# Gated linear attention into a squared-ReLU layer: k and q transposed by DMA from the fourth unit on, and the front of each unit issued ahead of the back of its predecessor

## Chip, cores, metric

One core of one Trainium2 chip. Its engines go by the names of the profile: PE (TensorE), PEld (PE's weight loads), DVE (VectorE), ACT (ScalarE), POOL (GpSimd) and SP, whose queue issues the DMAs. The releaser of a wait is what ended it. The metric is the device time of one execution in microseconds; the kernel before takes 197.5 us (median of 3 runs, 196.7 to 198.2).

## The reference

```python
# attention: 4 batches, 8 heads, 768 steps, head dimension 48
for t in range(S):
    state = alpha[:, :, t, :, None] * state + einsum('bhd,bhe->bhde', k[:, :, t], v[:, :, t])
    y[:, :, t] = einsum('bhd,bhde->bhe', q[:, :, t], state)
x = y.transpose(0, 2, 1, 3).reshape(3072, 384)
# layer ("MoE" in the code, one expert)
out = square(maximum(x @ w_in, 0)) @ w_out        # 384 -> 2048 -> 384
```

## The kernel before

The recurrence is done in chunks. A *unit* is 256 steps of one batch: 128 partitions, two steps (`j`) per partition, the halves of the partitions being two chunks (`ab`). There are 12 units, and for each an equal slice of the layer. Every operation is given to a list scheduler with a modelled cost, a priority and the buffers that it reads and writes; the scheduler fixes one order for each engine, and the engines then run in that order and wait by semaphores.

Within one unit: alpha's halves are multiplied (DVE), logarithm (ACT), a matmul with a triangle sums the columns (PE), exponentials (ACT) scale k and q (DVE), k and q are transposed on PE into a PSUM bank and copied out (DVE), scores (PE), mask (DVE), product with v and with the carried state (PE), then the output is transposed (PE) into the layout that the layer needs.

```python
psH = [128, 2, 512] FP32     # layer, first product: 2 banks
psP = [128, 2, 512] FP32     # scores, and the column sums: 2 banks
psO = [128, 512] FP32        # layer, second product
psT = [128, 1024] BF16       # every transpose: 1 bank
psY = 2 x [128, 512] FP32

def attention(u):
    # ... alpha's halves multiplied (DVE, line 485), logarithm into the single buffer lab (ACT, 487)
    def m1(pe):                                              # column sums, into the score banks
        pe.matmul(psP[:, 0, 0:HD], LBLK[:], lab)
        # ... five small ones
    # ... exponentials of psP into asb (ACT, 512)
    for t in range(2):                                       # t = 0: k, t = 1: q
        # ... qks[t] = raw[t] * asb[t]  (DVE, 522)
        def tr(pe, t=t):                                     # 8 transposes (PE, 533)
            pst = psT[:, :].rearrange("p (n a j s) -> p n a j s", n=NPR, a=2, j=2)
            for j in range(2):
                for p in range(NPR):
                    ins = pe.matmul(pst[:, p, :, j, :], QKS[qs][:, t, j, 2*p:2*p+2, :]..., IDENT[:], is_transpose=True)
        add("pe", tr, ...)
        add("dve", copy psT -> KQT[kt][:, t], 640, ...)      # line 540
    # ... kv: new state (PE, 551; DVE, GpSimd)
    # ... score: 2 x 16 matmuls of 64x64 into psP (PE, 586); mask (DVE, 593)
    def y(pe):
        # carried state: 128-column stationary, one matmul per head pair and chunk (605)
        pe.matmul(psY[ab][:, p*96:p*96+96], KQT[kt][:, 1, p, ab, :], st[:, p*96:p*96+96], ...)
        # ... 32 matmuls with v (612)
    # ... output out of psY (ACT, 624), 6 transposes into psT (PE, 630), copy (DVE, 636)

for u in range(U):
    if u >= NRAW: loads(u)
    attention(u)                 # the order in which operations are told decides who waits for whom
for m in range(U):
    moe(m, [2*m, 2*m+1])
```

Of the kernel before, what the change touches and what calls it, by code (L numbers as in the profile page):

```python
# [4 lines left out]
AF = mybir.ActivationFunctionType  # L5
FP32 = mybir.dt.float32
BF16 = mybir.dt.bfloat16
# [275 lines left out]
def act_ns(n):  # L283
    return 65 + n * 0.8333
# [6 lines left out]
def bass_gla_recurrent__then__act_relu_squared_kernel(  # L291
# [9 lines left out]
    B, H, S, D = q.shape  # L301
    HD = H * D
    DM, DFF = moe_w_in.shape
    assert H == 8 and D == 48 and DM == HD and B % 2 == 0
    C = 128
# [3 lines left out]
    NPR = H // 2  # L309
    DP = 64  # L310
    HP = C // 2
    units = [(b, c) for c in range(0, NCH, 2) for b in range(B)]
    U = len(units)
    G = 2 * U

    NRAW, NVR, NLAB, NASB, NQKS, NKQT, NPM, NV, NXB, NRR, NGT, NOSB = 3, 3, 1, 2, 2, 2, 4, 2, 4, 4, 4, 3

    def sb(name, shape, dt, n):
        return [nc.alloc_sbuf_tensor(f"{name}{i}", shape, dt) for i in range(n)]
# [4 lines left out]
    LAB = sb("lab", [128, 2, H, DP], BF16, NLAB)  # L324
    ASB = sb("asb", [128, 2, HD], BF16, NASB)
    QKS = sb("qks", [128, 2, 2, H, DP], BF16, NQKS)
    KQT = sb("kqt", [128, 2, NPR, 2, C], BF16, NKQT)
    PM = sb("pm", [128, 2, 2, 2 * C], BF16, NPM)
    VBF = sb("vbf", [128, 2, HD], BF16, NV)
    SBD = sb("sbd", [128, HD], BF16, 2 * B)  # L330
# [2 lines left out]
    ACM = sb("acm", [128, 2, H], FP32, 2)  # L333
    XBF = sb("xbf", [128, HD], BF16, NXB)
    XT = nc.alloc_sbuf_tensor("xt", [128, KT, G * C], BF16)
    LBLK = nc.alloc_sbuf_tensor("lblk", [128, 128], BF16)
# [18 lines left out]
    psH = nc.alloc_psum_tensor("psH", [128, 2, 512], FP32)  # L355
    psP = nc.alloc_psum_tensor("psP", [128, 2, 512], FP32)
    psO = nc.alloc_psum_tensor("psO", [128, 512], FP32)
    psT = nc.alloc_psum_tensor("psT", [128, 1024], BF16)
    psY = [nc.alloc_psum_tensor(f"psY{i}", [128, 512], FP32) for i in range(2)]

    pr = Program(nc)
    add = pr.add
    P = 7000.0
# [96 lines left out]
    def loads(u):  # L460
        b, c = units[u]
        t0 = c * C
        r, vr = u % NRAW, u % NVR
        for o, (dst, t, nm, key) in enumerate(((RAW[r][:, 2, :, :], alpha, "a", ("raw", r, 2)),
                                               (RAW[r][:, 0, :, :], k, "k", ("raw", r, 0)),
                                               (RAW[r][:, 1, :, :], q, "q", ("raw", r, 1)),
                                               (RAV[vr][:], v, "v", ("rav", vr)))):
            src = t[b, :, t0:t0 + 2 * C, :].rearrange("h (p j) d -> p h (j d)", j=2)
            chain("sp", lambda e, dst=dst, src=src: e.dma_start(dst, src), 400, 2 * u * P - 4 * P + o, writes=[key],  # L469
                name=f"ld{nm}{u}", dma=f"{nm}{vr if nm == 'v' else r}", lag=1240)  # L470

    def attention(u):
        b, c = units[u]
        t0 = c * C
# [6 lines left out]
        def heads(t):  # L481
# [13 lines left out]
        add("pool", lambda e: e.tensor_tensor(q0, q0, heads(RAL[0][:]), ALU.mult), 1000, pu + 520,  # L495
            reads=[("raw", r, 1), ("ral",)], writes=[("raw", r, 1)], name=f"mq{u}")

        def m1(pe):
            pe.matmul(psP[:, 0, 0:HD], LBLK[:], lab)
            col = psP[:, 0, HD:HD + 2 * H]  # L500
            pe.matmul(col, HSEL[:], HCOL[:], start=True, stop=False, skip_group_check=True)
            col = col.rearrange("p (a n) -> p a n", a=2)
            for p in range(NPR):
                ins = pe.matmul(col[:, :, 2 * p:2 * p + 2],  # L504
                                LAB[la][:, 0, 2 * p:2 * p + 2, :].rearrange("p h d -> p (h d)"), ONES4[:],
                                start=False, stop=True, skip_group_check=True)
            return ins

        add("pe", m1, pe_ns(HD) + 135, pu + 300,
            reads=[("lab", la), ("lblk",), ("ones",), ("hsel",), ("hcol",)], writes=[("ps", "P")], name=f"m1_{u}")  # L510
        for t, sc in ((0, -1.0), (1, 1.0)):
            add("act", lambda e, t=t, sc=sc: e.activation(ASB[a][:, t, :], psP[:, 0, 0:HD], AF.Exp, scale=sc),  # L512
                act_ns(HD), pu + 500 + t, reads=[("ps", "P")], writes=[("asb", a, t)], name=f"e{t}{u}")
        add("act", lambda e: e.activation(ACM[u % 2][:].rearrange("p a n -> p (a n)"), psP[:, 0, HD:HD + 2 * H],
                                          AF.Exp), 110, pu + 505, reads=[("ps", "P")],
            writes=[("acm", u % 2)], name=f"ec{u}")
        add("act", lambda e: e.activation(VBF[vb][:].rearrange("p j (h d) -> p h j d", h=H),  # L517
                                          RAV[vr][:].rearrange("p h (j d) -> p h j d", j=2), AF.Copy), act_ns(2 * HD), pu + 600,
# [2 lines left out]
        for t in range(2):  # L521
            add("dve", lambda e, t=t: e.tensor_tensor(  # L522
                QKS[qs][:, t, :, :, 0:D].rearrange("p j h d -> p h j d"),
                RAW[r][:, t, :, :].rearrange("p h (j d) -> p h j d", j=2),
                bass.AP(tensor=ASB[a], offset=t * HD, ap=[[2 * HD, 128], [D, H], [0, 2], [1, D]]), ALU.mult),
                1100, pu + 1500 + 400 * t, reads=[("raw", r, t), ("asb", a, t)], writes=[("qks", qs, t)],
                name=f"qk{t}{u}")

            def tr(pe, t=t):
                pst = psT[:, :].rearrange("p (n a j s) -> p n a j s", n=NPR, a=2, j=2)  # L530
                for j in range(2):
                    for p in range(NPR):
                        ins = pe.matmul(pst[:, p, :, j, :],  # L533
                                        QKS[qs][:, t, j, 2 * p:2 * p + 2, :].rearrange("p h d -> p (h d)"),
                                        IDENT[:], is_transpose=True)
                return ins

            add("pe", tr, pe_ns(*[128] * 8), pu + 2500 + 600 * t, reads=[("qks", qs, t), ("ident",)],
                writes=[("ps", "T")], name=f"tr{t}{u}")
            add("dve", lambda e, t=t: e.tensor_copy(KQT[kt][:, t, :, :, :].rearrange("p n a s -> p (n a s)"),  # L540
                                                    psT[:, :]), 640, pu + 3000 + 600 * t,
                reads=[("ps", "T")], writes=[("kqt", kt, t)], name=f"et{t}{u}")

        halves = range(1 if last else 2)

        def kv(pe):
# [28 lines left out]
        for hp in range(2):  # L575
            pm = (2 * u + hp) % NPM
            pb, key = (psH, [("ps", "H", 0), ("ps", "H", 1)]) if u == 0 and hp else (psP, [("ps", "P")])

            def score(pe, hp=hp, pb=pb):
                for i in range(2):  # L580
                    p = 2 * hp + i
                    for j in range(2):
                        for ab in range(2):
                            for h in range(2):
                                ro = slice(64 * h, 64 * h + 64)
                                ins = pe.matmul(pb[ab * HP:(ab + 1) * HP, h, (2 * i + j) * C:(2 * i + j + 1) * C],  # L586
                                                KQT[kt][ro, 0, p, ab, j * HP:(j + 1) * HP],
                                                KQT[kt][ro, 1, p, ab, :])
                return ins

            add("pe", score, 340, pu + 3800 + 10 * hp, reads=[("kqt", kt, 0), ("kqt", kt, 1)], writes=key,
                name=f"p{hp}{u}")
            add("dve", lambda e, pm=pm, pb=pb: e.tensor_tensor(  # L593
                PM[pm][:].rearrange("p h i s -> p (h i) s"),
                pb[:, :, :].rearrange("p h (i s) -> p (h i) s", i=2),
                bass.AP(tensor=MASK, offset=0, ap=[[2 * C, 128], [0, 4], [1, 2 * C]]), ALU.mult), 1170, pu + 4200,
                reads=key + [("mask",)], writes=[("pm", pm)], name=f"pm{hp}{u}")

        def y(pe):
            for ab in range(2):  # L600
                if first and ab == 0:
                    continue
                st = SBA[u % 2] if ab else SBD[old]
                for p in range(NPR):
                    pe.matmul(psY[ab][:, p * 96:p * 96 + 96], KQT[kt][:, 1, p, ab, :], st[:, p * 96:p * 96 + 96],  # L605
                              start=(p == 0), stop=False, skip_group_check=True)
            for h in range(H):
                pm = PM[(2 * u + h // 4) % NPM]
                for j in range(2):
                    for ab in range(2):  # L610
                        ro = slice(ab * HP, (ab + 1) * HP)
                        ins = pe.matmul(psY[ab][:, h * D:(h + 1) * D], pm[ro, h % 2, (h // 2) % 2, j * C:(j + 1) * C],  # L612
                                        VBF[vb][ro, j, h * D:(h + 1) * D],
                                        start=(first and ab == 0 and h == 0 and j == 0), stop=(j == 1),
                                        skip_group_check=True)
            return ins
# [91 lines left out]
    for step in ("u0", "u1", "i0", "i1", "i2", "i3", "o0", "o1", "o2", "o3", "u2"):  # L708
# [4 lines left out]
            w_in_piece(i, -1e5 + i)  # L713
        else:
            w_out_piece(i, -1e5 + 10 + i)
    for u in range(U):
        if u >= NRAW:
            loads(u)
        attention(u)
    for m in range(U):  # L720
        moe(m, [2 * m, 2 * m + 1])
    pr.schedule()
# [30 lines left out]
```

## Time and profile before

| | before |
|---|---|
| span of the profiled run | 194.2 us |
| PE busy / not busy | 185.8 / 8.4 us |
| PE not busy from 38 to 76 us | 1.3 us |
| steady unit | 14.37 us, PE without a gap |
| DMA queue: bytes, share of 16 engines | 29.89 MB, 51.9% |

The rows come from the page (busy times, DMA queue) and from the busy time by stretch; the steady unit is the distance of two starts of the product with v, 101.96 and 116.33 us. The prediction shows the other lines. Those of the operations removed, from the groups by line (engine, operation, out<-in, shapes, count, then busy us, mean ns, idle before and releaser):

```profile
L540 DVE COPY kqt<-psT 128x1024 bf16<-128x1024 bf16 x24 | 16.5, 686 | 5.8 <-PE psT L533 5.6
...
L533 PE MATMUL psT<-ident,qks 128*128 128x128 bf16 x192 | 14.7, 219 | 0.3 <-DVE qks L522 0.3
```

### The profile page before, as it was taken

To read this page: it belongs to the slowest core of one execution; us is meant where nothing else is said; L and a number is where in the kernel's file an instruction comes from. 1 tells how busy PE (TensorE), PEld (TensorE's weight loads), DVE (VectorE), ACT (ScalarE), POOL (GpSimd) and SP (SyncE) were. 2 spreads that over 40 slices of the span, in tenths; PEclk is the share of its full clock that TensorE was granted. 3 is DMA by queue.
4 is the path that set the end of the run, shared out by engine and by line. 5 is a ranking of instruction groups with operands and counts; after the bars stand their busy time and mean duration, and the time that the engine had idled before them with its cause. 6 is when DMAs were issued, how large, how long until landed. Compare 5 with 4: busy or idle time off the path is not lost.

```text
span 194.2 us, 5455 instructions
## 1 busy us (share of the span) xinstructions
PE 185.8 (96%) x2347; PEld 132.8 (68%) x2347; DVE 117.9 (61%) x172; ACT 129.5 (67%) x252; POOL 86.1 (44%) x97
## 2 busy tenths in 40 slices
PE   7999899899998999999999999999999999999994
PEld 2455676675775678778778778777777677687762
DVE  6698644795983875855855855836736727622230
ACT  2647898696777488658658559559459458277642
POOL 8243785272471473743742742822812812325000
PEclk9999999999999999999999999999999999999999
DMA  6999999999994670950950940910110110110112
GB/s 161 323 367 384 378 365 254 261 291 315 296 316 117 178 230 3 243 165 3 241 167 0 263 146 5 271 55 1 43 43 3 40 44 0 44 40 3 40 40 81
DMA packets 57111, 30.23 MB, mean 156 GB/s; under 512 B 50432, under 2 KB 55552, under 8 KB 57088
## 3 DMA queue, kind: packets, MB, share of 16 engines
q1 hardware_dynamic: 57088, 29.89, 51.9%
q8 instruction: 18, 0.29, 0.6%
q14 instruction: 5, 0.04, 0.1%
HBM read 25.17 MB, written 4.72 MB: 154 GB/s over the span
## 4 chain that ended last, share of the span: by engine, by line
PE 70%; DMA 11%; SPq 9%; ACT 4%; POOL 2%; DVE 1%; issue 1%
PE psH L663 27%; PE psO L693 26%; SPq L469 8%; DMA stg<-in_moe_w_in_dram 5%; PE psT L533 4%; DMA raw<-in_alpha_dram 3%; DMA rav<-in_v_dram 3%; PE psP L586 3%; PE psY L551 2%; PE psY L612 2%; PE psT L630 2%; PE psY L605 1%; PE psH L693 1%; POOL gt L679 1%; ACT rr L672 1%; SPq L435 1%
## 5 line engine op out<-in xcount | busy, mean ns | idle before, releaser
L679 POOL TENSOR_TENSOR gt<-rr 128x512 bf16<-128x512 bf16 x45 | 48.3, 1074 | 68.3 <-ACT rr L672 68.3
L663 PE MATMUL psH<-xt,win 128*128 128x256 bf16 x576 | 73.0, 273 | 1.1 <-ACT rr L672 1.1
L693 PE MATMUL psO<-wout,gt 128*128 128x384 bf16 x368 | 69.6, 326 | 1.1 <-ACT osb L701 0.7
L672 ACT ACTIVATE rr<-psH 128x512 bf16<-128x512 f32 x96 | 56.5, 600 | 16.2 <-PE psH L663 15.4
L663 PEld LDWEIGHTS psH<-xt,win 128*128 128x128 bf16 x576 | 53.4, 98 | 11.6 <-ACT rr L672 2.0
L693 PEld LDWEIGHTS psO<-wout,gt 128*128 128x128 bf16 x368 | 33.9, 98 | 19.8 <-ACT osb L701 0.9
L593 DVE TENSOR_TENSOR pm<-psP,mask 128x1024 bf16<-128x1024 f32 x23 | 28.1, 1220 | 13.6 <-PE psP L586 13.6
L679 DVE TENSOR_TENSOR gt<-rr 128x512 bf16<-128x512 bf16 x28 | 16.2, 580 | 22.5 <-ACT rr L672 22.4
L701 ACT ACTIVATE osb<-psO 128x384 f32<-128x384 f32 x23 | 11.3, 493 | 26.6 <-PE psO L693 26.5
L522 DVE TENSOR_TENSOR qks<-raw,asb 128x768 bf16<-128x768 f32 x24 | 23.9, 1028 | 4.5 <-ACT asb L512 4.5
L540 DVE COPY kqt<-psT 128x1024 bf16<-128x1024 bf16 x24 | 16.5, 686 | 5.8 <-PE psT L533 5.6
L495 POOL TENSOR_TENSOR raw<-raw,ral 128x384 f32<-128x384 f32 x12 | 12.9, 1073 | 13.8 <-ACT ral L490 13.6
L636 DVE COPY xt<-psT 128x768 bf16<-128x768 bf16 x12 | 6.7, 556 | 14.1 <-PE psT L630 14.1
L533 PE MATMUL psT<-ident,qks 128*128 128x128 bf16 x192 | 14.7, 219 | 0.3 <-DVE qks L522 0.3
L676 ACT ACTIVATE gt<-rr 128x512 bf16<-128x512 bf16 x23 | 14.6, 636 | 0.5
L624 ACT ACTIVATE xbf<-psY 128x384 bf16<-128x384 f32 x24 | 10.4, 487 | 6.0 <-PE psY L612 6.0
L533 PEld LDWEIGHTS psT<-ident,qks 128*128 128x128 bf16 x192 | 12.2, 98 | 3.2 <-DVE qks L522 1.3
L487 ACT ACTIVATE lab<-raw 128x768 bf16<-128x768 f32 x12 | 10.4, 864 | 6.0 <-DVE raw L485 6.0
L386 PE MATMUL psO<-warm 128*128 128x512 bf16 x43 | 13.1, 441 | 1.3 <-DVE warm L377 1.3
L485 DVE TENSOR_TENSOR raw<-raw 128x384 f32<-128x384 f32 x12 | 7.6, 630 | 6.7 <-DMA raw<-in_alpha_dram 6.7
L512 ACT ACTIVATE asb<-psP 128x384 bf16<-128x384 f32 x24 | 10.6, 495 | 1.3 <-PE psP L504 1.3
L517 ACT ACTIVATE vbf<-rav 128x768 bf16<-128x768 f32 x12 | 10.2, 848 | 1.5 <-DMA rav<-in_v_dram 1.5
(59 smaller groups left out, 154.2 us busy)
## 6 DMA issues: line engine op xcount, KB each, us to landing
raw<-in_alpha_dram SPq DMA_DIRECT2D x12, 384.0 KB, 5.6
raw<-in_k_dram SPq DMA_DIRECT2D x12, 384.0 KB, 4.2
raw<-in_q_dram SPq DMA_DIRECT2D x12, 384.0 KB, 4.8
rav<-in_v_dram SPq DMA_DIRECT2D x12, 384.0 KB, 5.2
out_dram<-osb SPq DMA_DIRECT2D x24, 192.0 KB, 2.1
stg<-in_moe_w_in_dram SPq DMA_DIRECT2D x4, 768.0 KB, 8.0
stg<-in_moe_w_out_dram SPq DMA_DIRECT2D x4, 768.0 KB, 7.5
```

The lines of the kernel that those rows point to most:

```text
L386: o = Op("pe", lambda pe: pe.matmul(psO[:, 0:512], WARM[:, 0:128], WARM[:], start=not begun, stop=True, skip_group_check=True), 216, 0, "w")
L469: chain("sp", lambda e, dst=dst, src=src: e.dma_start(dst, src), 400, 2 * u * P - 4 * P + o, writes=[key], name=f"ld{nm}{u}", dma=f"{nm}{v ...
L495: add("pool", lambda e: e.tensor_tensor(q0, q0, heads(RAL[0][:]), ALU.mult), 1000, pu + 520, reads=[("raw", r, 1), ("ral",)], writes=[("ra ...
L522: add("dve", lambda e, t=t: e.tensor_tensor(QKS[qs][:, t, :, :, 0:D].rearrange("p j h d -> p h j d"), RAW[r][:, t, :, :].rearrange("p h (j ...
L533: ins = pe.matmul(pst[:, p, :, j, :], QKS[qs][:, t, j, 2 * p:2 * p + 2, :].rearrange("p h d -> p (h d)"), IDENT[:], is_transpose=True)
L540: add("dve", lambda e, t=t: e.tensor_copy(KQT[kt][:, t, :, :, :].rearrange("p n a s -> p (n a s)"), psT[:, :]), 640, pu + 3000 + 600 * t, ...
L593: add("dve", lambda e, pm=pm, pb=pb: e.tensor_tensor(PM[pm][:].rearrange("p h i s -> p (h i) s"), pb[:, :, :].rearrange("p h (i s) -> p (h ...
L663: ins = pe.matmul(psH[:, hb, i * n:(i + 1) * n], WIN[:, kk, fj * 128:(fj + 1) * 128], XT[:, kk, g0 * C:g0 * C + n], start=(kk == 0), stop= ...
L672: add("act", lambda e, hb=hb, rb=rb: e.activation(RR[rb][:], psH[:, hb, :], AF.Relu), act_ns(512), pu + 600, reads=[("ps", "H", hb)], writ ...
L676: add("act", lambda e, sq=sq, dst=dst: e.activation(dst, sq, AF.Square), 560, pu + 1200, reads=[("rr", rb)], writes=[("gt", gt, u)], name= ...
L679: add(how, lambda e, sq=sq, dst=dst: e.tensor_tensor(dst, sq, sq, ALU.mult), {"dve": 560, "pool": 1100}[how], pu + 1200, reads=[("rr", rb) ...
L693: ins = pe.matmul(po, GT[gt][:, fj, ti * C:(ti + 1) * C], WOUT[:, fj, :], start=(fj == 0), stop=(fj == FT - 1))
```

## The change

The intent: take the transposes of k and q off PE, the engine that sets the end, and give them to the DMA engines, half idle after 62 us. A DMA is slower to answer (4.1 us at the median after the change), so the *front* of a unit (up to the scaled and transposed k and q) is told to the scheduler before the *back* (state, scores, products, output) of the unit before. Line numbers after the change are 5 to 17 higher: column sums 506, scaling 529, DMA transpose 537, state 566, scores 601, mask 608, carried state 621, product with v 629, output transposes 647, layer 680 and 710. The diff, cut to its core:

```diff
-    NLAB = 1
+    NLAB = 2
-    KQT = sb("kqt", [128, 2, NPR, 2, C], BF16, NKQT)
+    KQT = sb("kqt", [128, 2, 2, NPR, C], BF16, NKQT)
-    psT = nc.alloc_psum_tensor("psT", [128, 1024], BF16)
+    psTF = nc.alloc_psum_tensor("psTF", [128, 512], FP32)
+    psT = psTF[:].bitcast(BF16)
+    AHEAD_FROM = 3
+    M1_FROM = 3
+    XBAR_FROM = (3, 3)
+        pa, pakey = (psTF[:], ("ps", "T")) if u >= M1_FROM else (psP[:, 0, :], ("ps", "P"))
         def m1(pe):
-            pe.matmul(psP[:, 0, 0:HD], LBLK[:], lab)
+            pe.matmul(pa[:, 0:HD], LBLK[:], lab)
             # ... exponentials read pa
+            if u >= XBAR_FROM[t]:
+                add("sp", lambda e, t=t: e.dma_start_transpose(
+                    KQT[kt][:, t, :, :, :].rearrange("p j n s -> p (j n) s"),
+                    QKS[qs][:, t, :, :, :].rearrange("p j h d -> p (j h d)")), 1500, -2e6 + u, reads=[("qks", qs, t)],
+                    writes=[("kqt", kt, t)], name=f"x{t}{u}", dma=f"kq{kt}{t}", lag=1700)
+                continue
             # ... transposes on PE as before, in the new layout
+        yield                                   # front above, back below
         # ... scores: moving operand KQT[kt][ro, 1, :, p, ab*HP:(ab+1)*HP], two runs of 64
-                    pe.matmul(psY[ab][:, p * 96:p * 96 + 96], KQT[kt][:, 1, p, ab, :], st[:, p * 96:p * 96 + 96],
+                    for j in range(2):
+                        pe.matmul(psY[ab][j * HP:(j + 1) * HP, p * 96:p * 96 + 96],
+                                  KQT[kt][:, 1, j, p, ab * HP:(ab + 1) * HP], st[:, p * 96:p * 96 + 96],
-    for u in range(U):
-        if u >= NRAW:
-            loads(u)
-        attention(u)
+    parts = [attention(u) for u in range(U)]
+    for u in range(U + 1):
+        if u < U:
+            if u >= NRAW:
+                loads(u)
+            if not (u and u < AHEAD_FROM):
+                next(parts[u], None)            # front of u
+        if u:
+            next(parts[u - 1], None)            # back of u - 1
+            if u < AHEAD_FROM:
+                next(parts[u], None)
```

So there are four parts: the DMA transposes, the order, the move of the column sums into the transpose bank (with a second log buffer), and the layout, which splits the carried-state product in two column halves.

More of the change, by code (lines that the diff above doesn't have):

```diff
@@ L314, in bass_gla_recurrent__then__act_relu_squared_kernel @@
     G = 2 * U
-    NRAW, NVR, NLAB, NASB, NQKS, NKQT, NPM, NV, NXB, NRR, NGT, NOSB = 3, 3, 1, 2, 2, 2, 4, 2, 4, 4, 4, 3
+    NRAW, NVR, NLAB, NASB, NQKS, NKQT, NPM, NV, NXB, NRR, NGT, NOSB = 3, 3, 2, 2, 2, 2, 4, 2, 4, 4, 4, 3
     def sb(name, shape, dt, n):
@@ L496, in attention @@
             reads=[("raw", r, 1), ("ral",)], writes=[("raw", r, 1)], name=f"mq{u}")
+        pa, pakey = (psTF[:], ("ps", "T")) if u >= M1_FROM else (psP[:, 0, :], ("ps", "P"))
         def m1(pe):
-            pe.matmul(psP[:, 0, 0:HD], LBLK[:], lab)
-            col = psP[:, 0, HD:HD + 2 * H]
+            pe.matmul(pa[:, 0:HD], LBLK[:], lab)
+            col = pa[:, HD:HD + 2 * H]
             pe.matmul(col, HSEL[:], HCOL[:], start=True, stop=False, skip_group_check=True)
@@ L509, in attention @@
         add("pe", m1, pe_ns(HD) + 135, pu + 300,
-            reads=[("lab", la), ("lblk",), ("ones",), ("hsel",), ("hcol",)], writes=[("ps", "P")], name=f"m1_{u}")
+            reads=[("lab", la), ("lblk",), ("ones",), ("hsel",), ("hcol",)], writes=[pakey], name=f"m1_{u}")
         for t, sc in ((0, -1.0), (1, 1.0)):
-            add("act", lambda e, t=t, sc=sc: e.activation(ASB[a][:, t, :], psP[:, 0, 0:HD], AF.Exp, scale=sc),
-                act_ns(HD), pu + 500 + t, reads=[("ps", "P")], writes=[("asb", a, t)], name=f"e{t}{u}")
-        add("act", lambda e: e.activation(ACM[u % 2][:].rearrange("p a n -> p (a n)"), psP[:, 0, HD:HD + 2 * H],
-                                          AF.Exp), 110, pu + 505, reads=[("ps", "P")],
+            add("act", lambda e, t=t, sc=sc: e.activation(ASB[a][:, t, :], pa[:, 0:HD], AF.Exp, scale=sc),
+                act_ns(HD), pu + 500 + t, reads=[pakey], writes=[("asb", a, t)], name=f"e{t}{u}")
+        add("act", lambda e: e.activation(ACM[u % 2][:].rearrange("p a n -> p (a n)"), pa[:, HD:HD + 2 * H],
+                                          AF.Exp), 110, pu + 505, reads=[pakey],
             writes=[("acm", u % 2)], name=f"ec{u}")
@@ L527, in attention @@
                 name=f"qk{t}{u}")
+            if u >= XBAR_FROM[t]:
[4 more added lines that the diff above has]
+                continue
             def tr(pe, t=t):
-                pst = psT[:, :].rearrange("p (n a j s) -> p n a j s", n=NPR, a=2, j=2)
+                pst = psT[:, :].rearrange("p (j n s) -> p j n s", j=2, n=NPR)
                 for j in range(2):
                     for p in range(NPR):
-                        ins = pe.matmul(pst[:, p, :, j, :],
+                        ins = pe.matmul(pst[:, j, p, :],
                                         QKS[qs][:, t, j, 2 * p:2 * p + 2, :].rearrange("p h d -> p (h d)"),
@@ L539, in attention @@
                 writes=[("ps", "T")], name=f"tr{t}{u}")
-            add("dve", lambda e, t=t: e.tensor_copy(KQT[kt][:, t, :, :, :].rearrange("p n a s -> p (n a s)"),
+            add("dve", lambda e, t=t: e.tensor_copy(KQT[kt][:, t, :, :, :].rearrange("p j n s -> p (j n s)"),
                                                     psT[:, :]), 640, pu + 3000 + 600 * t,
                 reads=[("ps", "T")], writes=[("kqt", kt, t)], name=f"et{t}{u}")
+        yield
         halves = range(1 if last else 2)
@@ L586, in score @@
                                 ins = pe.matmul(pb[ab * HP:(ab + 1) * HP, h, (2 * i + j) * C:(2 * i + j + 1) * C],
-                                                KQT[kt][ro, 0, p, ab, j * HP:(j + 1) * HP],
-                                                KQT[kt][ro, 1, p, ab, :])
+                                                KQT[kt][ro, 0, j, p, ab * HP:(ab + 1) * HP],
+                                                KQT[kt][ro, 1, :, p, ab * HP:(ab + 1) * HP])
                 return ins
@@ L604, in y @@
                 for p in range(NPR):
-                    pe.matmul(psY[ab][:, p * 96:p * 96 + 96], KQT[kt][:, 1, p, ab, :], st[:, p * 96:p * 96 + 96],
-                              start=(p == 0), stop=False, skip_group_check=True)
+                    for j in range(2):
+                        pe.matmul(psY[ab][j * HP:(j + 1) * HP, p * 96:p * 96 + 96],
+                                  KQT[kt][:, 1, j, p, ab * HP:(ab + 1) * HP], st[:, p * 96:p * 96 + 96],
+                                  start=(p == 0), stop=False, skip_group_check=True)
             for h in range(H):
```

## The prediction

> **What bounds the kernel now.** I read the page's busy shares first, then the chain of work that ended last, then the chain in order of time for one unit, then the busy time by stretch, and last who waits for whom. The shares and the chain:
>
> ```profile
> PE 185.8 (96%) x2347; PEld 132.8 (68%) x2347; DVE 117.9 (61%) x172; ACT 129.5 (67%) x252; POOL 86.1 (44%) x97
> ...
> PE 70%; DMA 11%; SPq 9%; ACT 4%; POOL 2%; DVE 1%; issue 1%
> ```
>
> TensorE (PE) is busy 96% of the span. A busy PE alone proves little (matmuls are pipelined, and 13.1 us of it are warm-up matmuls early on), but the chain is PE for 70%. The DMA and SP shares belong to the start: up to about 38 us the chain passes through input and weight loads. By stretch (us from the start, then busy time of PE, PEld, DVE, ACT, POOL, then clock, DMA share, GB/s):
>
> ```profile
> 38.00:50.00 12.00, 11.64 (x166) 8.20 (x164) 9.09 (x14) 9.90 (x20) 5.61 (x5) 1.00 1.09 302
> 50.00:62.00 12.00, 11.95 (x178) 9.02 (x176) 8.29 (x13) 8.21 (x17) 6.51 (x6) 1.00 0.93 257
> 62.00:76.00 14.00, 13.11 (x188) 9.70 (x187) 10.16 (x15) 9.37 (x19) 7.00 (x7) 1.00 0.52 143
> ...
> 104.55:118.92 14.37, 14.37 (x198) 10.83 (x196) 9.44 (x14) 9.97 (x21) 7.21 (x8) 1.00 0.49 139
> ...
> 147.80:162.29 14.49, 14.49 (x189) 10.74 (x188) 8.28 (x11) 9.87 (x21) 6.64 (x7) 1.00 0.08 28
> ```
>
> From 76 us on PE has no idle time, at full clock. One unit takes 14.4 us and no other engine is over 10.9 of that. DMA is loaded at 0.9 to 1.0 up to 62 us and at half or less afterwards. So PE work removed from the steady part should come off the end, until the next engine binds: ACT at 9.97 us a unit leaves room for over 4 us. The same unit in the chain (start, duration, what):
>
> ```profile
> 107.18 0.45 PE psT L533 x8
> 107.63 0.45 PE psY L551 x16
> 108.07 0.76 PE psO L693 x4
> 108.83 0.45 PE psT L533 x8
> 109.28 0.66 PE psH L663 x6
> ...
> 110.58 0.35 PE psP L586 x16
> ...
> 116.06 0.34 PE psY L605 x8
> 116.40 0.50 PE psY L612 x32
> 116.90 1.42 PE psH L663 x12
> ```
>
> The reader is to see two pieces of eight transposes (L533), 0.45 us each, both on the path. Because PE is pipelined I take the pieces, 56 ns per transpose, and not the 219 ns that the groups give as the length of one record: records overlap.
>
> **What the Trainium skill says.** (1) "TensorE: Matmul & The Clock Gate", Part 4 (PE-mode transpose): the output goes to PSUM, so a VectorE copy must follow, and one transpose costs about 275 ns in a kernel, 390 ns alone. The trace agrees on the copy (L540) but not on the price: 219 ns per record and 56 ns in a stream. The smaller figure is what can be saved. (2) "Advanced Engine Details and Errata", X-Bar Transpose (TRN2): transposing DMAs are as fast as regular ones. (3) "DMA: Bandwidth & Descriptors", Latency and other measured facts: 261 GB/s effective for a DMA transpose with a non-contiguous middle dimension. The trace of the kernel before has no such DMA, so neither is confirmed; an estimate from that figure is 0.26 MB / 261 GB/s = 1.0 us for one of the new transfers. (4) The same page, Rules for kernel authors: two transposing streams in flight must be serialized, while a transpose beside ordinary DMAs needs nothing. All new transposes come from the one SP queue, so I see no added wait there.
>
> **The change part by part.**
>
> Removed from PE: 16 transposes a unit in units 3 to 11, nine units. Two pieces of 0.45 us make 0.90 us a unit, 8.1 us in all, on the path.
>
> Removed from VectorE: two PSUM copies a unit (L540, 686 ns), 18 x 0.686 = 12.3 us. DVE is not the bound (9.4 of 14.4 us), so this gives nothing directly; it makes the score evictions and the two scaling products less likely to be late.
>
> Added to SP and the DMA engines: two transposes a unit, each 128 x 1024 bf16, 256 KB. The program's own model allows 1.5 us to issue, about 1.2 us of start, 1.7 us of transfer and 0.9 us of completion. For the ordinary 384 KB load the same model gives 1.2 + 1.24 + 0.9 = 3.3 us, and the fastest load in the trace landed in 3.3 us, so I trust it roughly: 5.3 us from a free SP to landing. The route replaced is shorter: in this unit 6.4 us from the first column-sum matmul (104.12) to the first score (110.51), of which transposes, copies and their waits take some 3.5 us. The new one should need 9 to 10 us. That latency is hidden if enough MoE matmuls stand between, and the unit period of over 13 us has them; the second half of the change (the front issued ahead, its first matmul in the transpose bank rather than in the score bank, a second log buffer) is there to make that room.
>
> Added to PE: with the new layout the carried-state product (L605) is split in two column halves: 16 matmuls instead of 8 in units 4 to 11, 8 instead of 4 in units 0 to 3. Today 8 take 0.34 us, 42 ns each. The halves occupy different columns of the array and should overlap, as the half-row matmuls of L551 do: 0.45/16 = 28 ns each at the same 96 columns. Then 16 take 0.45 us, +0.11 us a unit: 8 x 0.11 + 4 x 0.05 = 1.1 us. With no overlap at all, 16 x 42 = 0.68 us, +0.34, 3.4 us in all. I take 1.1. The score matmuls keep their number and size; their moving operand is two runs of 64 instead of one of 128, for which I charge nothing.
>
> Contention early: the transposes of units 3 and 4 fall at about 45 to 65 us, where DMA is loaded at 0.93. Four of them move 1.05 MB; at the 257 GB/s of that stretch they hold the loads up by 4 us (an estimate from that row). DVE waits there already for an alpha load that it meets ahead of the scaling products:
>
> ```profile
> DVE raw L485 <- DMA raw<-in_alpha_dram: 6.1, 3, 2.9
> ...
> PE psO L693 <- ACT osb L701: 0.7, 1, 0.7
> PE psY L551 <- ACT vbf L517: 0.6, 1, 0.6
> ```
>
> (Waits between 38 and 76 us: total, times, longest.) The 2.9 us on DVE reach PE as less than 1 us now, since MoE matmuls fill in. I charge 1.0 us for a longer wait here and for scores that find their transpose not yet landed later on.
>
> Sum: 197.5 - 8.1 + 1.1 + 1.0 = 191.5 us, a gain of 3%. The steady unit should fall from 14.4 to about 13.6 us.
>
> **The rivals.** (a) The transposes land late. The order of each engine is fixed from modelled costs; if a transpose takes 2 us more than modelled, in-order PE stops at the score matmuls of each unit. For it: the trace has no such DMA to check the model against, SP also waits in order for output tiles (up to 10 us at a time), and loads took 5 us at the median against 3.3 at best. Against it: the loads fit the model when the queue is free, DMA is half idle after 62 us, and the front runs ahead. With 1 us lost per unit the gain is gone: 197 to 200 us. With half of that, 195. (b) The early DMA phase lengthens and its delay is carried to the end, because PE runs dry around 50 to 65 us: a loss of 3 to 4 us, 194 to 195. For it: the DVE wait above; against it: the MoE backlog, and that the threshold at the fourth unit keeps the fullest stretch free of transposes. (c) PE stays the bound and everything is hidden, and the looser dependencies also remove the 1.3 us of PE idle that the first three stretches show: 189 to 190. (d) The column halves don't overlap: 2.3 us more than in my sum, 194. ACT or DVE as new bound I rule out: 10 and 8 us of a 13.6 us unit.
>
> **Range and chances.** My value lies between (c) and the mixture of (a), (b) and (d). Full hiding gives 188 to 190, one of the mild losses 193 to 196, and I round the value to 191.6 with 187.8 to 196.5 as the range. Two per cent faster means below 193.6: all but one of the four must go well, or at most one of (b) and (d) in part. I give that 0.70, within 2% 0.24, and slower by over 2% (over 201.5, which needs (a) in each of nine units at over 1 us) 0.06.
>
> **What would show it.** Right: no transposes by PE after unit 2 (48 instead of 192), a steady unit of 13.5 to 13.8 us with PE idle under 0.3 us in it, 16 carried-state matmuls in 0.4 to 0.5 us, SP issuing 18 transposes of 256 KB at about 1.5 us each, landing within 3 to 5 us. Wrong: PE idle before the score matmuls with the transposing DMA as releaser (rival a), a PE gap between 45 and 65 us behind a load (b), or carried-state matmuls at 0.6 to 0.7 us a unit (d). If the DMA's issue on SP takes several us, or its landing over 6 us, my latency was mis-sized and the time lies above 195 us.

## The result

| | median | runs | ratio to before, 95% |
|---|---|---|---|
| before | 197.65 us | 196.7 to 198.2, 4 runs | |
| changed | 191.44 us (190.76 of the three fast runs) | 190.0, 190.8, 192.1, and one of 350.1 | 0.967 (0.959 to 0.975) |

Ratios here are the mean time of one kernel's fast runs over that of the other's of the same rounds, so they are not quite the ratios of the medians quoted. The outputs are right.

The first profiled execution fell on the run of 350 us, with a span of 348.4 us. Its group of the layer's first product:

```profile
L680 PE MATMUL psH<-xt,win 128*128 128x256 bf16 x576 | 143.9, 438 | 0.0
```

These matmuls take twice their busy time of before (143.9 against 73.0 us for the same 576). It begins before any of the change has run: the first 15 warm-up matmuls take 7.06 us where e1 below takes 5.37, the next seven 3.27 where e1 takes 1.67. So the quickening that e1 shows within its first 7 us never came, and PE was slow for a whole execution. The views print a granted clock of 1.000 for it, but that is no measurement: this trace has no clock record (its page lacks the PEclk row), and 1.000 is what is printed then. The traces of e4 and e6 lack it too and ran at the usual speed. The state was not seen again: one of the 40 executions of kernels with transposing DMA, none of the 39 without (27 of them the kernel before). So few can't tell whether it has to do with the change; it is left out of every comparison. The profile after is that of run e1, the same kernel once more. Its page:

```profile
PE 179.0 (94%) x2283; PEld 124.9 (66%) x2283; DVE 115.8 (61%) x155; ACT 130.0 (68%) x252; POOL 84.6 (45%) x97
...
q1 hardware_dynamic: 76096, 34.61, 70.7%
...
PE 65%; DMA 13%; SPq 10%; ACT 6%; DVE 2%; issue 1%; POOL 1%; DVEq 0%
...
kqt<-qks SPq DMA_TRANSPOSE x18, 4.1
```

PE has 6.8 us less to do, while its time not busy grew from 8.4 to 10.8 us (span less busy). There are 18 new DMAs, 4.1 us each at the median from issue to landing. Where PE stands still, by stretch (PE is the first busy time after the length):

```profile
38.00:50.00 12.00, 10.95 (x176) 7.86 (x177) 11.20 (x15) 10.69 (x22) 6.87 (x6) 1.00 1.07 289
50.00:62.00 12.00, 10.35 (x110) 7.32 (x107) 9.26 (x11) 8.96 (x18) 6.86 (x6) 1.00 1.09 233
62.00:76.00 14.00, 12.96 (x217) 9.49 (x217) 9.59 (x13) 9.23 (x20) 5.72 (x6) 1.00 1.09 255
...
102.41:115.99 13.58, 13.58 (x193) 10.04 (x190) 10.15 (x12) 10.06 (x22) 7.19 (x7) 1.00 0.83 187
```

From 38 to 76 us PE is idle 1.05 + 1.65 + 1.04 = 3.7 us, where it was 1.3 before; that 2.4 is the whole growth. In the steady part there is no gap, and a unit takes 13.58 us in place of 14.37. The steady unit in the chain of work, for comparison with the chain in the prediction:

```profile
111.15 0.35 PE psP L601 x16
...
112.91 0.16 PE psTF L506
...
113.18 0.35 PE psP L601 x16
...
115.59 0.46 PE psY L621 x16
```

The two pieces of 0.45 us are gone. The carried-state piece (L621) has grown from 0.34 to 0.46 us. And the column sums of the next unit (L506) stand *between* the two score groups of this one, which they could not in the score bank.

The two profiled executions differ by 4.4 us in span, while the two ratios, 0.967 here and 0.969 in e1, say 6.6 and 6.2 us (3.3 and 3.1%). The profiled execution of before was a quick one, 196.4 us, where its 27 executions reach from 196.0 to 200.5; I take 6.2 to 6.6 us as the gain and the 4.4 as what these two traces can account for.

### The profile page after: what moved, and what is told of

It is laid out like the page before. It is cut to its first block, busy times and chain, and to the rows that moved or that the text cites. A ratio compares the mean times of both kernels' runs of the same rounds, so it can differ in the third digit from the quotient of the medians.

```text
span 348.4 us, 5330 instructions
## 1 busy us (share of the span) xinstructions
PE 344.3 (99%) x2283; PEld 183.2 (53%) x2283; DVE 100.3 (29%) x155; ACT 134.8 (39%) x252; POOL 81.6 (23%) x97
## 3 DMA queue, kind: packets, MB, share of 16 engines
HBM read 25.17 MB, written 4.72 MB: 86 GB/s over the span
## 4 chain that ended last, share of the span: by engine, by line
PE 99%; ACT 0%; DVE 0%; issue 0%
PE psH L680 39%; PE psO L710 37%; PE psO L387 6%; PE psP L601 3%; PE psY L629 2%; PE psTF L647 2%; PE psY L566 2%; PE psY L621 2%; PE psH L710 2%; PE psTF L547 2%; PE psTF L506 1%; PE psP L506 0%; PE psTF L511 0%; ACT osb L718 0%; PE psH L601 0%; PE psP L511 0%
## 5 line engine op out<-in xcount | busy, mean ns | idle before, releaser
L680 PE MATMUL psH<-xt,win 128*128 128x256 bf16 x576 | 143.9, 438 | 0.0
L710 PE MATMUL psO<-wout,gt 128*128 128x384 bf16 x368 | 138.7, 554 | 0.0
L680 PEld LDWEIGHTS psH<-xt,win 128*128 128x128 bf16 x576 | 79.5, 142 | 52.9 <-issue 13.6
L710 PEld LDWEIGHTS psO<-wout,gt 128*128 128x128 bf16 x368 | 49.7, 140 | 58.6 <-issue 50.0
L387 PE MATMUL psO<-warm 128*128 128x512 bf16 x43 | 21.0, 660 | 1.3 <-DVE warm L378 1.3
L653 DVE COPY xt<-psTF 128x768 bf16<-128x768 bf16 x12 | 6.7, 558 | 53.4 <-PE psTF L647 53.4
L693 ACT ACTIVATE gt<-rr 128x512 bf16<-128x512 bf16 x23 | 14.5, 629 | 0.4
L601 PE MATMUL psP<-kqt 64*64 64x128 bf16 x368 | 13.0, 277 | 0.0
L586 POOL TENSOR_TENSOR sbd<-tmp,acm 128x384 bf16<-128x384 f32 x8 | 6.9, 862 | 24.4 <-DVE tmp L584 24.4
L601 PEld LDWEIGHTS psP<-kqt 64*64 64x64 bf16 x368 | 6.4, 111 | 10.3 <-issue 10.2
L647 PEld LDWEIGHTS psTF<-perm,xbf 128*128 128x128 bf16 x72 | 9.0, 151 | 4.4 <-issue 1.9
L647 PE MATMUL psTF<-perm,xbf 128*128 128x128 bf16 x72 | 11.2, 327 | 0.0
```

The costliest lines, as they stand in the source:

```text
L387: o = Op("pe", lambda pe: pe.matmul(psO[:, 0:512], WARM[:, 0:128], WARM[:], start=not begun, stop=True, skip_group_check=True), 216, 0, "w")
L586: add("pool", lambda e, dst3=dst3, acm=acm, ab=ab: e.tensor_tensor(dst3, TMP[ab][:].rearrange("p (n d) -> p n d", d=D), acm, ALU.mult), 10 ...
L601: ins = pe.matmul(pb[ab * HP:(ab + 1) * HP, h, (2 * i + j) * C:(2 * i + j + 1) * C], KQT[kt][ro, 0, j, p, ab * HP:(ab + 1) * HP], KQT[kt][ ...
L647: ins = pe.matmul(psT[:, (2 * i + ab) * 128:(2 * i + ab + 1) * 128], XBF[xb][:, i * 128:(i + 1) * 128], PERM[:], is_transpose=True)
L680: ins = pe.matmul(psH[:, hb, i * n:(i + 1) * n], WIN[:, kk, fj * 128:(fj + 1) * 128], XT[:, kk, g0 * C:g0 * C + n], start=(kk == 0), stop= ...
L693: add("act", lambda e, sq=sq, dst=dst: e.activation(dst, sq, AF.Square), 560, pu + 1200, reads=[("rr", rb)], writes=[("gt", gt, u)], name= ...
```

## The experiments

PE busy and idle are those of each profiled execution (idle is span less busy). Busy counts a matmul's record to its end, so the same work in more scattered pieces shows a little more. e1 to e4 ran on one chip, e5 to e9 on another, e10 to e14 on a third; each was timed against before on its own chip. Medians are of all runs, ratios of the fast ones alone. Slow were one run of e3 (211.8 us), two of e4 (201.5 and 201.8, beside 197.3 and 198.7), two of e5 (221.9 and 222.2) and one of e13 (193.3).

| run | median us | ratio to before (95%) | PE busy | PE idle |
|---|---|---|---|---|
| before | 197.3 to 197.9 | 1 | 185.8 | 8.4 |
| e1 the change again | 191.13 | 0.969 (0.960 to 0.977) | 179.0 | 10.8 |
| e2 order and bank, PE transposes | 202.17 | 1.022 (1.015 to 1.029) | 188.9 | 11.9 |
| e3 DMA transposes alone | 209.04 | 1.058 (1.051 to 1.065) | 184.5 | 23.1 |
| e4 layout alone | 200.12 | 1.003 (0.993 to 1.012) | 187.0 | 9.6 |
| e5 DMA transposes and bank | 220.99 | 1.115 (1.102 to 1.127) | 186.6 | 31.8 |
| e6 DMA transposes and order | 195.75 | 0.998 (0.992 to 1.003) | 180.2 | 13.6 |
| e7 all from the sixth unit | 193.24 | 0.986 (0.979 to 0.993) | 180.8 | 10.3 |
| e9 each transpose twice | 200.50 | 1.020 (1.013 to 1.028) | 180.6 | 17.0 |
| e10 small transposes in units 3, 4 | 189.85 (wrong) | 0.961 (0.954 to 0.967) | 178.6 | 9.8 |
| e12 k alone by DMA | 201.10 | 1.019 (1.013 to 1.025) | 184.6 | 14.5 |
| e13 alpha held back | 190.35 | 0.964 (0.957 to 0.970) | 177.7 | 10.9 |
| e14 e2 with alpha held back | 198.45 | 1.006 (0.999 to 1.013) | 186.6 | 9.7 |

### e1, e4: what PE saved

e1 is the changed kernel without an edit. e4 keeps only the layout:

```diff
-    NLAB = 2;  AHEAD_FROM = 3;  M1_FROM = 3;  XBAR_FROM = (3, 3)
+    NLAB = 1;  AHEAD_FROM = 12; M1_FROM = 12; XBAR_FROM = (12, 12)
```

> The changed kernel once more, unedited: three of its four runs took 190.0 to 192.1 us, one took 350 us with every matmul at about twice its usual duration, from the first warm-up matmul on. Theory (steady PE bound, 0.9 us of transposes a unit removed): 190 to 192 us, a steady unit of 13.4 to 13.7 us, PE idle under 0.3 us in it, 18 transposing DMAs landing 3 to 4 us after issue, carried-state product 0.4 to 0.5 us a unit. If the 350 us state belongs to the change (transposing DMA upsets something) it comes back in about one run of four; if it is a state of the chip it doesn't, or the kernel before shows it too.

> Only the new layout of the transposed k and q, so the carried-state product in two column halves (16 matmuls instead of 8) and scores with a moving operand of two runs of 64. Theory: 16 matmuls in 0.45 us, +0.11 us a unit, 198 to 199 us. Rival (halves do not overlap): +0.34 us a unit, 200 to 201 us.

e1 met its theory in every number but the landing, 3.1 to 6.1 us with a median of 4.1 in place of 3 to 4; the carried-state product took 0.46 us a unit. e4's four runs scatter from 197.3 to 201.8 us, two of them slow, and its ratio, 1.003, is not told apart from 1, so its time neither confirms nor refutes 1 us. Its trace does: PE busy is 187.0 against 185.8, 1.2 us more for the 80 added matmuls, and its steady unit 14.49 against 14.37. So the halves overlap. From e4 to e1 PE busy falls by 8.0 us, the price of the transposes. Why the product was split at all: the DMA writes each 128 rows as one run, so the 128 columns wanted lie in two runs of 64, and a try to give both to one matmul was refused by the build, which wants exactly one free dimension in the stationary operand.

### e2, e3: the parts alone

e2 sets only `XBAR_FROM = (12, 12)`; e3 only `AHEAD_FROM = 12`, `M1_FROM = 12` and `NLAB = 1`.

> Front issued ahead, first matmul in the transpose bank, two log buffers and the new layout, but k and q transposed on PE in all units. Theory (the gain is the PE time of the transposes): the unit keeps its 14.4 us plus about 0.1 for the split product, so 197 to 198.5 us, no gain. Rival (the gain comes from the order): 192 to 194 us.

> Transposes by DMA from the fourth unit on, but the old order of the parts, the first matmul in the score bank and one log buffer. Theory: the DMA's latency is hidden by over 13 us of unit period even without the new order, or mostly so, so 190 to 193.5 us. Rival (the order is what hides the latency): the scores come late, PE or the chain of a unit waits 1 to 3 us a unit, 197 to 205 us.

My theory fell in e3, and e2 did worse than either of its two. Neither part gains alone: the order costs 2%, the DMA transposes 6%, together they gain 3%. In e3 one unit takes 16.08 us, and PE is not busy for 1.7 of it. The timeline of e3, without the PE weight loads and the layer (start, duration, engine, line; in brackets idle before and releaser), then what PE waited for from 76 to 188 us (total, times, longest):

```profile
100.37 1.28 SPq L537 DMA_TRANSPOSE kqt<-qks  x1
...
102.33 2.07 SPq L537 DMA_TRANSPOSE kqt<-qks  x1
...
108.69 0.42 PE L601 MATMUL psP<-kqt 64*64 64x128 bf16 x16
...
110.44 0.42 PE L601 MATMUL psP<-kqt 64*64 64x128 bf16 x16 [0.29 <-DVE pm L608]
...
110.91 1.23 DVE L608 TENSOR_TENSOR pm<-psP,mask 128x1024 bf16<-128x1024 f32 x1 [0.53 <-PE psP L601]
...
113.82 0.34 PE L506 MATMUL psP<-lab,lblk 128*128 128x384 bf16 x1
```

```profile
PE psY L566 <- DVE qks L529: 5.0, 7, 0.9
PE psH L680 <- ACT rr L689: 1.3, 5, 0.3
PE psP L601 <- DVE pm L608: 1.2, 4, 0.3
```

The dependencies form a loop: transposes out at 100.4 to 104.4, scores at 108.7 and 110.4, masks to 112.1, and only then may the next unit's column sums (113.8) take the score bank; exponentials, scaling, and the next transpose goes out at 116.45, 16.08 us after the last. But the trace doesn't show this loop to be tight on the chip. The transpose of q landed at 106.8, 1.9 us before the scores (1.2 to 3.1 us in all units from 68 us on); no wait of PE between 76 and 188 us ends with a transpose; and the bank was free at 112.1, 1.7 us before the column sums took it. PE waits elsewhere, most at the state product for the scaled k. What is slow is the order. It is fixed beforehand from modelled costs, and in that plan the loop is real. e3's scheduler was run by itself, without a chip: it plans 16.4 us a unit for the middle of the program, and 14.1 for the kernel before. With the modelled latency of a transpose cut from 5.3 us to 4.1 (issue 1.4 us, transfer 0.6), the median that e1 measured, it plans 13.9 to 15.0, and with issue and transfer at 0.1 us each 13.6. So the likely cause is an order laid out for a latency that the model puts too high. No run tried the other order on the chip, so this is not shown.

### e5, e6: which dependency closes the loop

e5 sets only `AHEAD_FROM = 12`, e6 only `M1_FROM = 12`.

> Transposes by DMA, first matmul of the unit in the transpose bank and two log buffers, but each front issued after the back of its predecessor, as before. In the run with neither bank nor order the unit took 16.1 us, one turn of a loop: column sums, exponentials, scaling, DMA transpose, scores, masks, and only then, through the shared score bank, the next column sums. Theory A (the shared score bank closes the loop): with the bank moved the loop is open, 13.5 to 13.8 us a unit, 191 to 193 us. Theory B (the order of issue matters, since the transpose bank is also the bank of the predecessor's last transposes, which come after its scores): the loop stays closed, 15.5 to 17 us a unit, 205 to 213 us.

> Transposes by DMA, front issued ahead, two log buffers, but the first matmul in the score bank. Theory A (bank): the front's column sums must find the score bank free, so they stand either before both scores of the predecessor or after; with the order ahead they stand before, the loop is open too: 13.5 to 14.2 us a unit, 191 to 197 us. Theory B (bank and order are both needed): 15 to 16.5 us a unit, 203 to 212 us.

e5 is the slowest of all: theory B. Without the order, the column sums in the transpose bank wait for the predecessor's *last* use of it, the output transposes, which come after its scores and products. The timeline of e5:

```profile
119.19 0.56 DVE L653 COPY xt<-psTF 128x768 bf16<-128x768 bf16 x1 [2.80 <-PE psTF L647]
...
119.81 0.34 PE L506 MATMUL psTF<-lab,lblk 128*128 128x384 bf16 x1 [0.65 <-DVE xt L653]
```

A unit takes 16.75 us or more. That wait is 0.65 us a unit, though, and here too the transposes land early, 2.8 to 3.7 us before the scores from the fifth unit on: the planned order is slow, not the DMA. e6 changes the order: 195.75 us, theory A, though with products with v 7.4 to 20.6 us apart after 62 us and 2.8 us more PE idle than e1. So the order is what makes the transposes pay, and the bank on top of it gives the last 2.9% (0.998 to 0.969). Between e3 and e6 the log buffers went from one to two as well, and their share is not separated: with one, the order ahead is refused for a race. The second buffer alone didn't help in e5, which has it too.

### e14, e12: why the order alone loses

e14 is e2 with one dependency more (that of e13 below); e12 sets `XBAR_FROM = (3, 12)`.

> Only k is transposed by DMA from the fourth unit on; q stays on PE, so the transpose bank holds column sums, q's transposes and the last transposes of the unit. Theory (gain is the PE time of the pieces, 0.45 us each): half of the pieces, 9 x 0.45 = 4.05 us, come back, 194.5 to 196. Rival (what matters is the transpose bank: with any transposes through it the order ahead does harm, as in the run with all of them on PE, 202 us): 198 to 201.

> The run with the order alone (all transposes on PE, 202 us), with the alpha multiply held back as in the last attempt. In that run's trace DVE stands 3.1 us at the alpha multiply of a later unit, between the two maskings of unit 3; PE then stands 2.4 us and the clock of the stretch 50 to 62 us falls to 0.86. Theory (this wait in an in-order queue and the slow clock after it make up most of what the order alone loses, some 3.5 of 5 us): PE idle in that stretch under 1 us, clock 1.0, 198 to 199.5 us. Rival (the shared transpose bank makes the loss, in each unit): 201 to 203 us.

In e2 the loss starts with one wait. Its DVE timeline, then PE's, then the stretch (last numbers: clock, DMA share, GB/s):

```profile
56.80 0.62 DVE L490 TENSOR_TENSOR raw<-raw 128x384 f32<-128x384 f32 x1 [3.06 <-DMA raw<-in_alpha_dram]
57.35 1.21 DVE L608 TENSOR_TENSOR pm<-psP,mask 128x1024 bf16<-128x1024 f32 x1
```

```profile
58.62 0.45 PE L621 MATMUL psY<-sba,kqt 128*64 128x96 bf16 x8 [2.43 <-DVE pm L608]
...
59.75 2.64 PE L680 MATMUL psH<-xt,win 128*128 128x256 bf16 x12
```

```profile
50.00:62.00 12.00, 9.20 (x132) 6.74 (x130) 6.98 (x11) 6.50 (x12) 3.93 (x5) 0.86 1.03 282
```

The alpha multiply of a later unit stands on DVE ahead of a mask of unit 3, its load is late, DVE is in order, so mask and PE wait. After 2.4 us of rest PE's clock is down: the trace records half the clock for 3.41 us, and the same twelve matmuls that take 1.48 us take 2.64. The one run of e2 with a mean clock of 0.999 took 200.6 us, the others, at 0.991 and 0.992, 201.9 to 202.5. e14 moves that multiply, and this stretch of it reads

```profile
50.00:62.00 12.00, 11.67 (x175) 8.77 (x174) 9.00 (x14) 9.86 (x20) 6.34 (x6) 1.00 1.02 278
```

and the time falls to 198.45 us, the level of e4 (ratios 1.006 and 1.003). So e2's loss was this wait and its slow clock, not the shared bank, and the 1.2 us of PE of the split product; theory of e14. Without the wait, the order alone costs nothing that can be told from noise, and gains nothing. e12 had gone to the rival, 201.1 us, and by itself would have spoken for the bank, but its trace has the same wait of DVE, worse, and PE stands for a layer piece behind it:

```profile
DVE raw L490 <- DMA raw<-in_alpha_dram: 4.9, 1, 4.9
...
PE psO L710 <- DVE gt L696: 3.3, 1, 3.3
```

(waits of e12 from 46 to 62 us: total, times, longest), with a clock of 0.87 in the stretch. Its steady part also keeps small gaps, so e12 is not a clean measure of half the transposes.

### e10, e7, e13: the early idle of the change

e10 cuts the transposes of units 3 and 4 to 16 of 128 rows. e7 sets all three thresholds to 5. e13 holds the alpha multiply back:

```diff
# e10
-   KQT[kt][:, t, :, :, :]...,                      QKS[qs][:, t, :, :, :]...
+   KQT[kt][:, t, :, :, 0:(16 if u < 5 else C)]..., QKS[qs][0:(16 if u < 5 else C), t, :, :, :]...
# e13
-            pu - 500, reads=[("raw", r, 2)], writes=[("raw", r, 2)], name=f"aa{u}")
+            pu - 500, reads=[("raw", r, 2)], writes=[("raw", r, 2)], name=f"aa{u}", after=[scaled[u - 2]] if u > 4 else [])
```

> The changed kernel with the transposes of units 3 and 4 cut to 16 of 128 rows (one eighth of the bytes), the order on PE, DVE, ACT and GpSimd unchanged; its output for these units is wrong on purpose. Theory (the early PE idle of 3.7 us between 38 and 76 us, 2.4 over that before the change, comes from the four transposes competing with the loads): idle falls to 1.3 to 2 us and the time to 189 to 190. Rival (the order of issue itself brings it: the run with the order alone and no transposing DMA has 3.3 us there): idle stays at 3 to 4 us, 190.5 to 192.

> All three thresholds at the sixth unit in place of the fourth, so no transposing DMA before about 75 us, when the loads no longer fill the DMA engines. Theory (early contention costs some 2.4 us of PE idle between 38 and 76 us, against 1.3 before the change): that idle falls back to about 1.3 us, saving 2.4; two units more keep their 0.9 us of PE transposes, costing 1.8; so 190 to 191.5 us, a draw. Rival (the early idle has another cause, the order itself): idle stays at 3 to 4 us and the time is 192.5 to 194.

> An attempt at a better version: from the sixth unit on, the multiply of alpha's halves on DVE may stand only after the scalings of the unit two before, so that it no longer waits on DVE for a load ahead of them, and the two scalings stand back to back, so the transpose of q is issued about 1.4 us earlier. Theory (early DVE waits for loads cause part of the early PE idle): PE idle between 38 and 76 us falls by 1 to 2 us, 189 to 190.5 us. Rival (PE work alone sets the end and the rest is hidden): 190.5 to 192 us.

In e10 the order on PE, DVE, ACT and GpSimd is that of the change, so only the bytes differ. Its stretches:

```profile
50.00:62.00 12.00, 9.87 (x108) 7.09 (x106) 9.68 (x10) 9.29 (x18) 7.57 (x7) 1.00 0.95 254
62.00:76.00 14.00, 13.98 (x230) 10.36 (x228) 9.46 (x14) 10.13 (x21) 6.04 (x7) 1.00 0.63 174
```

With 0.59 us from 38 to 50, idle is 0.59 + 2.13 + 0.02 = 2.7 us against 3.7: the bytes of the four early transposes cost 1.0 us of PE (one trace each; the intervals of the two ratios overlap). It is between my two theories, nearer the rival: the other 1.4 us of the growth stay when the bytes are gone. What PE waits for then is mostly the squared input of the layer's second product, in two waits that read the same in e1 and e10:

```profile
PE psO L710 <- POOL gt L696: 1.1, 1, 1.1
PE psO L710 <- ACT gt L693: 1.0, 1, 1.0
```

e7 has 2.2 us there, so it pays less early, but 1.0 us of new gaps from 90 to 118 us, where its order changes over, and 1.8 us of transposes more on PE; 0.986 is worse than the change, not the draw that I expected. The fourth unit as threshold is the better of the two. e13 has 3.0 us of early idle (1.26 + 1.44 + 0.29), 0.7 less where I expected 1 to 2, and 190.35 us: its interval (0.957 to 0.970) overlaps that of the change (0.960 to 0.977), on another chip, so it is not shown to be faster.

### e9: how much slack the latency has

Each transpose is preceded by the same one into a scratch tile. Its modelled cost is 1 ns, so the order on PE, DVE, ACT and GpSimd stays that of the change.

```diff
+                add("sp", lambda e, t=t: e.dma_start_transpose(KQD[:, t, ...]..., QKS[qs][:, t, ...]...), 1, -2e6 + u - 0.5,
+                    reads=[("qks", qs, t)], writes=[("kqd", t)], name=f"xd{t}{u}", dma=f"kqd{t}", lag=1)
```

> Each transpose issued twice, the first into a scratch tile that nobody reads; the order of the instructions on all other engines is unchanged. The true transposes then land some 1.3 us (k) to 2.8 us (q) later and the DMA moves 4.7 MB more. In the changed kernel's trace q's transpose is issued at 105.6 us and the scores start at 111.1 us; with a landing of about 4.1 us the slack is about 1.4 us. Theory (slack small): scores wait about 1.4 us a unit, 14.5 to 15.5 us a unit, 200 to 206 us. Rival (latency well hidden): the unit stays at 13.6 us and only the early part grows, 192 to 194.5 us.

200.5 us, in the range of the theory, but not for the whole way. Its waits, then two stretches, each one unit long:

```profile
PE psP L606 <- DMA kqt<-qks: 7.9, 5, 3.0
```

```profile
93.58:108.49 14.91, 13.64 (x192) 10.02 (x188) 9.54 (x12) 10.05 (x21) 7.19 (x7) 1.00 0.95 205
150.26:163.85 13.59, 13.59 (x184) 9.79 (x181) 6.47 (x9) 9.12 (x20) 4.98 (x5) 1.00 0.49 107
```

While loads run, scores now wait for the transposes (five times, 7.9 us; in the change 0.3 us in all) and a unit takes up to 14.9 us; once the loads have ended, a unit is 13.59 us as in the change, twice the transposes or not. So the change is close to rival (a) of the prediction: some 1.3 to 2.8 us more of latency per unit (the estimate of the expectation above) and the gain is gone as long as loads run beside it. The traces agree: in the change the transpose of q landed 0.7 to 1.1 us before the scores in the three units between 97 and 125 us, and 2.3 to 3.3 us before them in the last three. e9 also adds 4.7 MB of traffic beside the loads, which no run separates from the latency.

## Why the prediction was right, step by step

- **PE sets the end.** Right: from 76 to 174 us PE has no gap, neither in the trace before nor in that of e1, so PE work taken away there comes off the end.
- **Transposes, 0.90 us a unit.** Right: PE busy falls by 8.0 us from e4 to e1, 8.1 forecast.
- **Column halves, +0.11 us a unit.** Right: 0.46 us for 16, +0.12, and 1.2 us of PE busy in e4 for the 1.1 forecast. Rival (d) is out.
- **Steady unit of 13.6 us.** Right, 13.58.
- **Early contention and late scores, 1.0 us.** Mis-sized: PE idle grew by 2.4 us between 38 and 76 us. Of it 1.0 is the four transposes' bytes (e10), which is the mechanism that I named. The other 1.4 stays without them, and what is left is mostly two waits of the layer's second product, 2.1 us together. They don't come with the order ahead alone: e14, with that order and without transposing DMA, has 0.7 us of idle in these stretches, and e13, the same with it, has 3.0. Why GpSimd and ACT are late there is open. Rival (b) was half there, 2.4 us in place of 3 to 4.
- **The sum.** -8.0 + 1.2 + 2.4 = -4.4 us, the difference of the two profiled spans; my sum was -6.0. The ratios say 6.2 to 6.6; of the difference, 1.3 us is that the profiled execution of before was quicker than the median of its runs (196.4 against 197.65). That my value came within 0.2 us of the recorded median is luck: the early term was off by 1.4 us, and the executions of one kernel differ by more.
- **"That latency is hidden if enough MoE matmuls stand between" and "the unit period of over 13 us has them".** The step failed as a reason, though not as a number. e3 has the same matmuls and a landing in time for the scores, and yet a unit takes 16.1 us: what counts is the order that the scheduler lays out for the modelled latency, with the loop through the score bank in it. The order ahead repairs that (e6), and the move of the bank with the second log buffer, which I took for a part of "making room", is a loss of its own without the order (e5). The new order is no mere help to the transposes; they gain nothing without it.
- **5.3 us from a free SP to landing.** Too long at the median: 4.1 us from the start of the issue to landing, 3.1 to 6.1, of which the issue on SP takes 1.4 (median). The slack that is left is small while loads run; e9 finds it used up by one more transpose.
- **VectorE loses 12.3 us of copies.** The copies went, yet DVE busy fell by only 2.1 us (117.9 to 115.8). The operations left became longer: the alpha multiply 862 ns at the mean, before 630; the k multiply 1009, before 775. In e1's trace the k multiply takes 1.39 us at 109.70 us, beside GpSimd multiplies, and 0.55 at 122.48, when GpSimd mostly stands still. The cause is likely that company; no run took it away.

## What to carry to other kernels

When a step on a busy engine is replaced by a slower one elsewhere, look for the loop from one iteration to the next that the step lies in, and add up that loop's latency. Where the order is fixed from modelled costs, look at the plan as well as at the trace: a loop that is too long in the model leaves a slow order behind, even when the chip is quicker than the model. Test each part of such a change alone and together: here the two parts cost 2% (most of it one wait that another order avoids) and 6% alone and gain 3% together. In an in-order queue, look what stands ahead of the operation that PE will need, and whether its data may be late.

## What the Trainium skill lacked or had wrong

- "Advanced Engine Details and Errata", X-Bar Transpose (TRN2), has transposing DMAs as fast as regular ones. Here the queue's share of the DMA engines went from 51.9% of 194.2 us to 70.7% of 189.8 us for 4.72 MB of transposes: 134.2 - 100.8 = 33.4 us of the 16 engines, 141 GB/s (an estimate, as loads slow each other too), where the plain traffic before has 29.89 MB / 100.8 us = 297 GB/s. The same sum for the second set in e9 (81.0% of 197.6 us) gives 182 GB/s. The 261 GB/s of "DMA: Bandwidth & Descriptors", Latency and other measured facts, was not reached either.
- No page gives what one 256 KB SBUF-to-SBUF transpose takes: 1.24 to 2.5 us on the SP queue (median 1.4), 3.1 to 6.1 us from the start of the issue to landing (median 4.1).
- "TensorE: Matmul & The Clock Gate", Part 4, has about 275 ns for a PE transpose in a kernel; the like figure here, the length of one record, is 219 ns. It doesn't give the cost in a stream, here 56 ns each in a run of eight.
- The same page, Part 1, has the clock fall after an idle window of some 3.4 us. In e2 a gap of 2.4 us was enough: the trace records half the clock for 3.41 us from the end of the gap, and twelve matmuls took 2.64 us in place of 1.48.
- The same page, Part 1, warns that the clock's trace events are unreliable, with a slow state of over 50 us. Here PE ran at half speed for a whole execution of 348 us, once in 79 executions, and the trace holds no clock event at all.
